# A decode kernel's layer crossing: half of a further V chunk kept on chip for each batch row, a key ring of 24 KB in place of 32 KB, and other places for the loads around it

## The chip, the cores and the metric

The kernel runs on one core of a Trainium2 chip. The metric is the device time of one execution in microseconds, the median of several runs of the same program. All data is float32.

## The reference

Two layers. Each adds to `x` (2 batch rows of one token, 512 channels) an attention over a cache, and then a small mixing MLP:

```python
x = x + _A_ref(_layernorm(x), A_k_cache, A_v_cache, A_wq, A_wo)
x = x + _B_ref(_layernorm(x), B_w1, B_b1, B_w2, B_b2)
# and both lines once more, on the same caches and weights
def _A_ref(x, k_cache, v_cache, wq, wo):      # Hq 32, Hkv 8, Sk 32768, Dh 128
    q = heads of (x @ wq);  k, v = each cached head for 4 query heads
    p = softmax(q k^T * Dh ** -0.5)
    return (p v) @ wo
def _B_ref(x, w1, b1, w2, b2):                # one token, F = 1792
    return w2 * gelu(w1 * layernorm(x) + b1) + b2
```

A cached head of one batch row is 32768 x 128 floats, 16.8 MB, in K and again in V. There are 16 such pairs. The second layer reads the same caches with other queries, and its queries need the whole result of the first layer for that batch row. So nearly everything is read from memory twice.

## The kernel before, in words

**Units and chunks.** A unit is one (layer, batch row, KV head); there are 32. Its K and its V are each eight chunks of 2 MB (16 KB in each of the 128 partitions), and a chunk is eight quads (256 KB, 2 KB per partition). For each K chunk TensorE makes scores (`scores`, L483), eight matmuls; after the last chunk the row maximum is taken (L498, L506, L508, L512), ScalarE makes the exponentials (L523, L540), and TensorE multiplies them with V (`acc`, L640), again eight matmuls for a chunk. TensorE takes each float32 matmul in two passes, so the trace shows 16 matmul records for a chunk where the program's list has eight instructions.

**Memory.** One tile `mem` holds everything that is streamed: cells of 16 KB per partition, numbered from 0, one chunk to a cell. Cells 9 to 12 are shared with the projection weights; behind cell 12 lie five further quads (`REST`, "cell 13"). Every cache load is one DMA that `load` (L191) puts on the single queue of SyncE (SP), in a fixed order written by the kernel's own planner. A load waits on SP for the last reader of the cell that it overwrites, and all later loads stand behind it.

**Units around the crossing.** Head 7 is the keeper. The order of the units there is, as (layer, batch row, head):

- unit 13 = `N1`: (0, 0, 7), the last of layer 0 for row 0
- unit 14 = `N1 + 1`: (0, 1, 5)
- unit 15 = `N1 + 2`: (1, 0, 7)
- unit 16 = `N2`: (0, 1, 7), the last of layer 0 for row 1
- unit 17 = `N2 + 1`: (1, 0, 5)
- unit 18 = `N3`: (1, 1, 7); unit 19: (1, 1, 5)

After unit 13 layer 0 is complete for row 0. While K of unit 14 streams, the mixer of row 0 is computed, chiefly on DVE and ACT (14 gelu tiles, `hidden_sum`), with a few products on TensorE (`mix_2` L755, `mix_3` L919, `to_columns` L366), and then the queries of unit 15 (`q_products`, L397, one product for each quarter of the channels). This is the first crossing. The second is the same for row 1, under K of unit 17. During a crossing the stream brings K alone.

**What stays on chip.** K chunks 0 to 2 of the keeper stay in cells 0 to 2 from layer 0 to layer 1. Of its V, `KEPT` names the places: chunks 1, 2, 3 in cells 8 to 10, chunks 5, 6, 7 in cells 3 to 5, and five quads of chunk 4 in cell 13 (three more of its quads go through PSUM). Chunk 0 is read again in layer 1. Both rows use the same places, one after the other.

**The ring.** With so much held, K of units 14 and 17 has two cells, 6 and 7. It is loaded in half chunks (four quads, 1 MB) into four slots of half a cell: 32 KB per partition in all. A load waits until TensorE has read the half chunk four before it. TensorE keeps this order, half chunk by half chunk, and between them come the mixer's products, the query products and idle products (`idle_products`, L799): matmuls of the identity, in sets of three, whose result nobody reads. V of the two units goes the same way for its first two chunks.

**Places.** Outside of the ring, `spread`, `buffer` and `half` choose a free cell for a load: the one that gives it the most time between its last reader and its own issue. `FOLLOWS` and `BETWEEN` are keys that place V chunks among the K chunks of the next unit in the load order.

## Time and profile before

| | |
|---|---|
| median of 3 runs | 2501.42 us (2501.13 to 2503.52) |
| the profiled execution | 2503.54 us, its span 2501.7 us |
| read from memory | 1061.19 MB, 424 GB/s over the span |
| busy share of the span | PE 57%, PE weight loads 16%, DVE 10%, ACT 7% |
| first crossing (K of unit 14) | about 1130 to 1190 us of the span |
| second crossing (K of unit 17) | about 1310 to 1370 us |

The page cuts the span into 40 slices of 62.5 us and gives for each the busy share of the 16 DMA engines and what they moved; the windows do the same for chosen stretches. In the timeline a row is a run of like instructions on one engine: its start, its length, the line, and in brackets the idle time ahead of it with what ended it.

### The profile page before, as it was taken

Reading aid. Unit: us, or ns where it says so; the run is one execution under the profiler, and the core shown is the slowest. Engines: PE = TensorE matmul, PEld = TensorE weight load, DVE = VectorE, ACT = ScalarE, POOL = GpSimd, SP = SyncE. Lnnn points to the kernel's source line nnn. Section 1 sums busy time; section 2 is a strip of 40 time slices with the busy share of each in tenths; the row PEclk is TensorE's granted clock in tenths of the full one; section 3 lists DMA queues with packets and bytes.
Section 4 is the critical chain, followed back from the end, with each engine's and each line's share of the span. In section 5 each row is a group of like instructions: output and inputs, shape, how many; then the busy total and the mean of one; then the engine's idle time right before and its main releaser. Section 6 shows DMA issues by size and latency. Waiting matters only on the chain.

```text
span 2501.7 us, 20938 instructions
## 1 busy us (share of the span) xinstructions
PE 1425.7 (57%) x9478; PEld 393.0 (16%) x9478; DVE 256.5 (10%) x659; ACT 185.5 (7%) x544; POOL 4.9 (0%) x17
## 2 busy tenths in 40 slices
PE   4544645546545545658578675455555565456546
PEld 1111111111111111113123111111111111111112
DVE  1000000000000000003123110000000000010002
ACT  0000000000000000002012000000000000012002
POOL 0000000000000000000000000000000000000000
PEclk8777677776777777879889888777777777777778
DMA  9999999999999999989999999999999999999996
GB/s 420 435 433 428 437 434 433 431 433 431 434 434 428 434 435 432 424 348 418 427 423 415 424 429 432 432 433 433 434 430 431 435 431 432 432 434 434 427 434 283
DMA packets 30882, 1062.54 MB, mean 425 GB/s; under 512 B 3781, under 2 KB 3785, under 8 KB 4426
## 3 DMA queue, kind: packets, MB, share of 16 engines
q1 hardware_dynamic: 30504, 1061.17, 98.7%
q8 instruction: 74, 1.21, 0.2%
q14 instruction: 14, 0.11, 0.0%
q10 hardware_dynamic: 290, 0.04, 0.0%
HBM read 1061.19 MB, written 0.00 MB: 424 GB/s over the span
## 4 chain that ended last, share of the span: by engine, by line
DMA 72%; PE 26%; issue 0%; another core or an unknown queue 0%; DVE 0%; ACT 0%; SPq 0%; ACTq 0%
DMA mem<-in_v_dram 60%; PE acc L640 19%; DMA mem<-in_kt_dram 11%; PE scores L483 3%; DMA mem<-in_wqo_dram 2%; PE kept L164 1%; PE kept L397 1%; PE small L799 1%; PE small L512 0%; PE small L671 0%; PE bcast L397 0%; PE kept L298 0%; SPq L191 0%; PE small L506 0%
## 5 line engine op out<-in xcount | busy, mean ns | idle before, releaser
L483 PE MATMUL scores<-mem,small_sb 128*32 128x512 f32 x4096 | 618.5, 725 | 549.1 <-DMA mem<-in_kt_dram 549.1
L640 PE MATMUL acc<-mem,S 128*16 128x512 f32 x4088 | 617.3, 736 | 469.5 <-DMA mem<-in_v_dram 465.9
L483 PEld LDWEIGHTS scores<-mem,small_sb 128*32 128x32 f32 x4096 | 147.3, 127 | 922.5 <-issue 838.4
L523 ACT ACTIVATE S<-S,small_sb 128x128 f32<-128x128 f32 x232 | 119.3, 518 | 1967.5 <-DVE small_sb L514 1378.6
L640 PEld LDWEIGHTS acc<-mem,S 128*16 128x16 f32 x4088 | 131.2, 109 | 829.2 <-issue 693.3
L498 DVE TENSOR_REDUCE small_sb<-scores 128x1 f32<-128x512 f32 x64 | 44.2, 691 | 755.0 <-PE scores L483 755.0
L518 DVE STREAM_TRANSPOSE S<-scores 128x512 f32<-128x512 f32 x64 | 45.5, 710 | 144.2 <-PE acc L640 140.0
L397 PE MATMUL kept<-mem,small_sb 128*2 128x512 f32 x96 | 52.8, 671 | 4.3 <-DMA mem<-in_wqo_dram 2.6
L298 PE MATMUL kept<-mem,small_sb 128*1 128x512 f32 (+1 forms) x236 | 43.1, 612 | 2.7 <-ACT mem L894 2.4
L523 ACT ACTIVATION_READ_ACCUMULATOR S<-S,small_sb 128x1 f32 x232 | 43.3, 187 | 0.0
L508 DVE TENSOR_REDUCE small_sb<-small 1x4 f32<-1x128 f32 x32 | 8.9, 279 | 282.1 <-PE small L506 282.1
L673 DVE RECIPROCAL small_sb<-small 128x4 f32<-128x4 f32 x32 | 5.9, 185 | 301.0 <-PE small L671 301.0
L682 DVE TENSOR_TENSOR small_sb<-small,small_sb 128x4 f32<-128x4 f32 x31 | 5.1, 164 | 293.9 <-PE small L680 293.9
L610 DVE SCALAR_TENSOR_TENSOR S<-acc,small_sb,S 128x128 f32<-128x128 f32 x93 | 32.6, 351 | 3.3
L894 ACT ACTIVATE S<-bcast,small_sb 128x512 f32<-128x512 f32 x28 | 21.6, 778 | 86.4 <-DVE small_sb L763 84.3
L799 PE MATMUL small<-small_sb 128*128 128x128 f32 x160 | 25.1, 297 | 1.0 <-DVE small_sb L371 1.0
L608 DVE TENSOR_SCALAR S<-acc,small_sb 128x128 f32<-128x128 f32 x31 | 10.8, 350 | 143.1 <-PE acc L640 143.1
L164 PE MATMUL kept<-mem,small_sb 48*2 48x512 f32 x32 | 25.3, 934 | 0.0
L423 PE MATMUL small<-small_sb,mem 2*128 2x2 f32 x112 | 14.7, 249 | 17.9 <-DVE mem L419 17.9
L799 PEld LDWEIGHTS small<-small_sb 128*128 128x128 f32 x160 | 21.0, 199 | 16.6 <-issue 15.4
L397 PE MATMUL bcast<-mem,small_sb 128*1 128x512 f32 (+1 forms) x40 | 20.3, 633 | 0.0
L680 PEld LDWEIGHTS small<-small_sb,S 128*128 128x128 f32 x62 | 12.5, 252 | 47.3 <-issue 39.7
(154 smaller groups left out, 348.0 us busy)
## 6 DMA issues: line engine op xcount, KB each, us to landing
mem<-in_kt_dram SPq DMA_DIRECT2D x12, 4096.0 KB
mem<-in_v_dram SPq DMA_DIRECT2D x23, 2048.0 KB
mem<-in_v_dram SPq DMA_DIRECT2D x9, 4096.0 KB
mem<-in_kt_dram SPq DMA_DIRECT2D x32, 1024.0 KB
mem<-in_kt_dram SPq DMA_DIRECT2D x12, 2048.0 KB
mem<-in_wqo_dram SPq DMA_DIRECT2D x4, 3840.0 KB
mem<-in_wqo_dram SPq DMA_DIRECT2D x3, 4096.0 KB
mem<-in_kt_dram SPq DMA_DIRECT2D x2, 6144.0 KB
```

What stands on the lines that cost most here:

```text
L164: nc.tensor.matmul(q_ps[n][:B, :], low[:, j * B : (j + 1) * B], lowered[h][:, j * D : (j + 1) * D], start=(j == 0), stop=False,)
L298: nc.tensor.matmul((rows if to is None else to)[32 * g : 32 * g + b + 1, :], weights if b else weights[:, 1:], row, start=to is not None, ...
L397: nc.tensor.matmul(q_ps[n][:m, :], xnT[:, d, b : b + m], wq_at(h, d), start=(d == 0 and h not in lowered), stop=(d == last),)
L423: nc.tensor.matmul(pt[:, r * m : (r + 1) * m], q_row[n][:m, r * DH : (r + 1) * DH], ident[:m, :m], start=True, stop=True,)
L483: nc.tensor.matmul(sc_ps[n, half][32 * g : 32 * g + 32, :], q, kc[k * NG + g], start=(i == 0 and k == 0), stop=(i == PACK - 1 and k == SUB ...
L498: nc.vector.tensor_reduce(mx[n][:, half : half + 1], sc_ps[n, half], axis=AX.X, op=ALU.max)
L518: nc.vector.transpose(S[half], sc_ps[n, half])
L523: nc.scalar.activation(s[:, :, h], s[:, :, h], AF.Exp, bias=neg[n][:, h : h + 1], scale=SCALE, accum_out=lsum[n][:, half, h : h + 1],)
L610: nc.vector.scalar_tensor_tensor(t, acc[:, k * DH : (k + 1) * DH], mask[:, k : k + 1], t, op0=ALU.mult, op1=ALU.add)
L640: nc.tensor.matmul(acc[32 * g : 32 * g + R * QT, :], S[half][:, col : col + R * QT], vc[q], start=(c == v_from[n] and q < NG), stop=(c == ...
L799: nc.tensor.matmul(p[:, :P], ident, ident, start=True, stop=True)
L894: nc.scalar.activation(hid[key, f], px[key], AF.Gelu_apprx_tanh, bias=shift[key][:, f : f + 1], scale=slope[key][:, f : f + 1],)
```

## The change

- `KEPT` becomes `KEPT_V`, one table for each row. Both get an entry for chunk 0: four of its eight quads stay in the upper half of cell 7. For row 0 the chunks 1 to 3 now stay in cells 3 to 5 and the chunks 5 to 7 in cells 8 to 10; row 1 has them as before.
- The ring for K of units 14 and 17 (`ring_quads`, a new function) is four slots of three quads (768 KB each), from cell 6 to the middle of cell 7: 24 KB per partition. A K group of 32 quads is loaded as ten pieces of three and one of two. Eleven quads of V go through it too; the other five of V chunk 1 go to cell 0.
- `PLACE_K` and a longer `PLACE_V` fix the cells of loads in units 13 to 20, which were chosen by the rules. K of units 16 and 19 is loaded one chunk at a time at its start (before: three chunks in one, or two).
- `FOLLOWS` and `BETWEEN` move some V chunks in the load order.
- The four query products of the next unit stand 1, 2, 1 behind three half chunks (before: 2, 2 behind two), and the copy of the query row comes half a chunk later. Of the eight sets of idle products in each crossing the three earliest stay.

SP's loads at the first crossing. Rows are groups of like DMAs; 128x2048 is four quads, 128x1536 three, 128x4096 a whole chunk. Before:

```order
L191 DMA mem<-in_v_dram 128x8192
L191 DMA mem<-in_v_dram 128x4096
L191 DMA mem<-in_v_dram 128x12288
L191 DMA mem<-in_v_dram 128x2560
L191 DMA mem<-in_v_dram 128x1536
L191 DMA mem<-in_v_dram 128x4096 x3
L191 DMA mem<-in_kt_dram 128x2048 x16
L191 DMA mem<-in_v_dram 128x2048 x4
L191 DMA mem<-in_v_dram 128x4096 x3
```

Now:

```order
L196 DMA mem<-in_v_dram 128x8192
L196 DMA mem<-in_v_dram 128x2048 x2
L196 DMA mem<-in_v_dram 128x12288
L196 DMA mem<-in_v_dram 128x2560
L196 DMA mem<-in_v_dram 128x1536
L196 DMA mem<-in_v_dram 128x4096 x3
L196 DMA mem<-in_kt_dram 128x1536 x10
L196 DMA mem<-in_kt_dram 128x1024
...
L196 DMA mem<-in_v_dram 128x1536 x3
L196 DMA mem<-in_v_dram 128x1024
L196 DMA mem<-in_v_dram 128x2560
L196 DMA mem<-in_v_dram 128x4096 x3
```

V chunk 0 of unit 13 comes in two halves, one of which stays; the 16 half chunks of K have become two times eleven pieces (the second eleven are like the first), and V of unit 14 follows in four pieces and a rest.

PE in the first crossing, from `mix_2` to the end of K. Rows are groups of matmuls; `scores` x4 is half a chunk. Before:

```order
L755 MATMUL bcast<-S_91,small_sb 128x512
L483 MATMUL scores<-mem,small_sb 32x512 x12
L799 MATMUL small<-small_sb 128x128 x3
L483 MATMUL scores<-mem,small_sb 32x512 x4
L799 MATMUL small<-small_sb 128x128 x3
...
L919 MATMUL bcast<-S_91,small_sb 128x512
L799 MATMUL small<-small_sb 128x128 x3
L483 MATMUL scores<-mem,small_sb 32x512 x4
L366 MATMUL small<-small_sb,S_91 128x1 x4
L799 MATMUL small<-small_sb 128x128 x3
L483 MATMUL scores<-mem,small_sb 32x512 x4
L397 MATMUL bcast<-mem,small_sb 1x512 x2
L799 MATMUL small<-small_sb 128x128 x3
L483 MATMUL scores<-mem,small_sb 32x512 x4
L397 MATMUL bcast<-mem,small_sb 1x512 x2
L799 MATMUL small<-small_sb 128x128 x3
```

Now:

```order
L797 MATMUL bcast<-S_91,small_sb 128x512
L518 MATMUL scores<-mem,small_sb 32x512 x16
L841 MATMUL small<-small_sb 128x128 x3
...
L961 MATMUL bcast<-S_91,small_sb 128x512
L518 MATMUL scores<-mem,small_sb 32x512 x4
L398 MATMUL small<-small_sb,S_91 128x1 x4
L518 MATMUL scores<-mem,small_sb 32x512 x4
L429 MATMUL bcast<-mem,small_sb 1x512
L518 MATMUL scores<-mem,small_sb 32x512 x4
L429 MATMUL bcast<-mem,small_sb 1x512 x2
L518 MATMUL scores<-mem,small_sb 32x512 x4
L429 MATMUL bcast<-mem,small_sb 1x512
```

The first four half chunks after `mix_2` stand bare (before: three), then three half chunks have a set of idle products behind them (one of them is shown), and behind `mix_3` there are none.

SP behind the last V load of unit 14 (the first row), between the crossings. Before:

```order
L191 DMA mem<-in_v_dram 128x4096
L191 DMA mem<-in_kt_dram 128x4096 x2
L191 DMA mem<-in_kt_dram 128x12288
L191 DMA mem<-in_v_dram 128x4096
L191 DMA mem<-in_kt_dram 128x4096
L191 DMA mem<-in_kt_dram 128x8192 x2
```

Now:

```order
L196 DMA mem<-in_v_dram 128x4096
L196 DMA mem<-in_kt_dram 128x4096 x5
L196 DMA mem<-in_v_dram 128x2048
L196 DMA mem<-in_kt_dram 128x4096
L196 DMA mem<-in_kt_dram 128x8192 x2
```

The first two of the K loads are the last of unit 15; then K chunks 0 to 2 of unit 16, in one before and now in three; then V chunk 0 of unit 15, now half of it; then K chunk 3 of unit 16. That last load goes to cell 10 by `PLACE_K`; before, the rule gave it cell 7, and the next load (chunks 4 and 5) cells 3 and 4.

The diff, cut to what the text speaks of:

```diff
-KEPT = {1: (8, 8), 2: (8, 9), 3: (8, 10), 4: (5, 13), 5: (8, 3), 6: (8, 4), 7: (8, 5)}
+KEPT_V = (
+    {0: (4, 7.5), 1: (8, 3), 2: (8, 4), 3: (8, 5), 4: (5, 13), 5: (8, 8), 6: (8, 9), 7: (8, 10)},
+    {0: (4, 7.5), 1: (8, 8), 2: (8, 9), 3: (8, 10), 4: (5, 13), 5: (8, 3), 6: (8, 4), 7: (8, 5)},
+)
-PLACE_V = {(1, 7): 1}
+PLACE_K = {(0, 6): 5, (2, 3): 0, (2, 4): 2, (2, 5): 0, (2, 6): 2, (2, 7): 6, (3, 3): 10, (3, 4): 3, (3, 6): 5, ...}
+PLACE_V = {(1, 2): 1, (1, 3): 2, (1, 4): 6, (1, 5): 1, (1, 6): 6, (1, 7): 1, (2, 0): 7, (2, 4): 8, ...}
-FOLLOWS = {2: (2.2, -0.9, -0.8, -0.7, 3.5, -0.6, -0.5, -0.4), 5: (3.05, 0.1, 0.2, 0.3, 5.1, 3.1, 3.2, 3.3)}
+FOLLOWS = {2: (2.2, -0.9, -0.8, -0.7, 3.5, -0.6, -0.5, -0.4), 5: (3.05, -0.9, -0.8, -0.7, 5.1, 3.1, 3.2, 3.3)}
-BETWEEN = (1.1, 1.2, 1.3, 2.1, 2.2, 3.1, 4.1, 5.1)
+BETWEEN = (2.1, 2.2, 2.3, 2.4, 2.5, 3.1, 4.1, 5.1)
+RING0, RING_SLOTS, RING_QUADS, RING_V = 6, 4, 3, 11
...
+    def ring_quads(n, is_v, c, count=JT // QT):
+        layer, b, h = unit_of(n)
+        c0, size = next(g for g in GROUPS if g[0] <= c < sum(g))
+        own = ring.setdefault((n, is_v, c0), [])
+        end = min(size * (JT // QT), RING_V if is_v else NCH * JT)
+        w = QT * P
+        a = piece(v if is_v else kt, b * HKV + h, c0, size)
+        while len(own) < (c - c0) * (JT // QT) + count:
+            f, slot = len(own), turns[0] % RING_SLOTS
+            turns[0] += 1
+            m = min(RING_QUADS, end - f)
+            k = RING0 * (JT // QT) + slot * RING_QUADS
+            t = mem[:, k * w : (k + m) * w]
+            load(t, a[:, f * w : (f + m) * w])
+            until = (v_done if is_v else k_done)[n, c0 + (f + m - 1) // (JT // QT)]
+            for j in range(k // NG, -(-(k + m) // NG)):
+                busy[j] = max(busy[j], until)
+            own += quads(t)
+        return own[(c - c0) * (JT // QT) :][:count]
...
+        elif n in (N1 + 1, N2 + 1):
+            k_at[n, c] = ring_quads(n, False, c)
+            return
         elif limit == RING:
-            bufs = spread(m, until, n in (N1 + 1, N2 + 1) and m == 1)
+            bufs = spread(m, until, False, PLACE_K.get((n - N1, c)))
...
-            loads = ((0, 3), (3, 1), (4, 2), (6, 2)) if n in (N1, N2) else ((0, 2), (2, 2), (4, 2), (6, 2))
+            loads = ((0, 3), (3, 1), (4, 2), (6, 2)) if n == N1 else ((0, 2), (2, 2), (4, 2), (6, 2))
+            if n in (N2, N3 + 1):
+                loads = (*((c, 1) for c in range(NG)), (4, 2), (6, 2))
...
-                q2 = mixed[layer - 1, b] + 0.5
-                q3 = q2 + 1
+                q2 = mixed[layer - 1, b] + 1
+                q3 = q2 + 0.5
...
-            for k in range(2, 2 * (NCH - 3)):
-                at(kend - 0.5 * k - 0.5, idle_products, KEEP_UP, rank=3)
+            for k in range(7, 2 * (NCH - 3)):
+                at(kend - 0.5 * k, idle_products, KEEP_UP, rank=3)
...
-            at(q, q_products, n + 1, 0, 1)
-            at(q + 0.5, q_products, n + 1, 2, 3)
+            at(q, q_products, n + 1, 0)
+            at(q + 0.5, q_products, n + 1, 1, 2)
+            at(q + 1, q_products, n + 1, 3)
```

More of the change, by code (lines that the diff above doesn't have):

```diff
@@ L192, in load, with buffer @@
         loaded[0] += t.shape[-1] / CK
[L194 to L196 removed]
+    def buffer(m, limit, until, place=None):
+        ks = range(0, limit - m + 1, m) if place is None else [place]
+        k = min(ks, key=lambda k: (-room(k, m, until), idle(k, m)))
         assert idle(k, m) <= now[0]
@@ L199, in buffer, with half @@
         return cells(k, m)
-    def half(until):
-        k = min((k / 2 for k in range(2 * WCELL0)), key=lambda k: (-fit(k, 0.5, until), idle(k, 0.5)))
+    def half(until, place=None):
+        ks = [k / 2 for k in range(2 * WCELL0)] if place is None else [place]
+        k = min(ks, key=lambda k: (-fit(k, 0.5, until), idle(k, 0.5)))
         assert fit(k, 0.5, until) >= 1
@@ L225, in spread @@
         k = min(ks, key=lambda k: (-fit(k, m, until), idle(k, m)))
-        if fit(k, m, until) >= 2 and not parted:
+        if (place is not None or fit(k, m, until) >= 2) and not parted:
+            assert idle(k, m) <= now[0] and fit(k, m, until) >= 1, (now, k, m, until, fit(k, m, until), lead(k, m), idle(k, m))
             hold(k, m, until)
@@ L576, in load_v @@
                 return
-            bufs = [half(until)[:, : CK - f]]
+            bufs = [half(until, PLACE_V.get((n - N1, c)) if layer else None)[:, : CK - f]]
+        elif n in (N1 + 1, N2 + 1) and c * (JT // QT) < RING_V:
+            at = ring_quads(n, True, c, min(JT // QT, RING_V - c * (JT // QT)))
+            f = len(at) * w
+            bufs = [cells(0)[:, : CK - f]] if f < CK else []
+            if bufs:
+                assert idle(0) <= now[0]
+                hold(0, 1, until)
         elif limit == RING:
```

24 lines of the change are left out of this document (13 added, 11 removed).

## The prediction

> **What bounds the kernel now.** I read the page first: the slices, the queues, the chain.
>
> ```profile
> DMA  9999999999999999989999999999999999999996
> GB/s 420 435 433 428 437 434 433 431 433 431 434 434 428 434 435 432 424 348 418 427 423 415 424 429 432 432 433 433 434 430 431 435 431 432 432 434 434 427 434 283
> q1 hardware_dynamic: 30504, 1061.17, 98.7%
> DMA 72%; PE 26%; issue 0%; another core or an unknown queue 0%; DVE 0%; ACT 0%; SPq 0%; ACTq 0%
> ```
>
> One queue is busy for 98.7% of the span and carries nearly all the bytes. The end is therefore set by two things: how many bytes there are at which rate, and the moments at which the queue has nothing to do. The moments lie in slices 18 to 23, around the two crossings; the rest runs at 430 or more. TensorE counts only where it lets a load go late. So I looked at windows there, the first row being the undisturbed stream:
>
> ```profile
> 500.00:950.00 450.00, 239.53 (x1562) 62.71 (x1554) 31.86 (x91) 23.66 (x88) 0.00 (x0) 0.75 1.00 433
> 1100.00:1120.00 20.00, 8.58 (x51) 2.45 (x51) 2.04 (x6) 3.62 (x10) 0.00 (x0) 0.74 0.50 216
> 1130.00:1165.00 35.00, 26.25 (x170) 9.75 (x170) 11.13 (x22) 8.25 (x11) 0.54 (x1) 0.85 1.00 420
> 1320.00:1355.00 35.00, 26.32 (x184) 9.76 (x177) 14.46 (x27) 10.01 (x13) 0.54 (x1) 0.90 1.01 419
> 1180.00:1200.00 20.00, 14.75 (x117) 4.96 (x120) 7.31 (x15) 1.38 (x3) 0.00 (x0) 0.90 1.00 389
> 1360.00:1380.00 20.00, 19.50 (x142) 7.49 (x142) 7.01 (x17) 1.39 (x3) 0.54 (x1) 1.00 1.00 394
> 1565.00:1570.00 5.00, 1.21 (x16) 0.23 (x12) 0.85 (x2) 0.00 (x0) 0.00 (x0) 0.81 0.95 380
> 1555.00:1565.00 10.00, 5.70 (x36) 1.23 (x32) 0.00 (x0) 0.00 (x0) 0.00 (x0) 0.66 1.02 437
> ```
>
> The last column is GB/s, the one ahead of it the DMA share. Large loads go at 433; the ring's half chunks at 420 with the engines full, so that rate belongs to the piece. The queue stands still for 10 us before 1120 (share 0.50 of 20 us). Behind the rings it loses 20 x (420 - 389) / 420 = 1.5 us and 20 x (420 - 394) / 420 = 1.2 us, and at 1565 5 x (437 - 380) / 437 = 0.65 us.
>
> **Bytes.** Half of V chunk 0 stays on chip for both rows.
>
> ```profile
> mem<-in_v_dram SPq DMA_DIRECT2D x23, 2048.0 KB
> mem<-in_kt_dram SPq DMA_DIRECT2D x32, 1024.0 KB
> ```
>
> A chunk of 2048 KB is 2.097 MB, 4.84 us at 433. Two halves fewer are 2.097 MB: **-4.84 us**. Against it, pieces get smaller. The two V chunks that now come in halves pay the step from 433 to 420: 4.2 MB, 0.3 us. For pieces of 768 KB no window stands alone. From 2 MB to 1 MB a piece cost 3%; if the same step came again at 768 KB it would be 13 GB/s on 2 x 16.8 MB, 2.5 us; nothing if the rate depends on the row of a partition only below that size. A quarter less is nearer to no step: I take 0.2 us. Bytes together: **-4.3 us** (-4.8 to -2.0).
>
> In a sentence that the sum can do without: the Trainium skill, DMA: Bandwidth & Descriptors, gives a load 2.0 us and its bytes at 436 GB/s, with the advice to make loads of 1 MiB at least; were that paid in a row, a K unit of the ring would go from 16 x 4.4 = 70 us to some 82. Here 1 MB pieces flow at 420, 2.5 us each, so the fixed part lies under the transfers queued ahead, as long as there are such.
>
> **The hole before 1120.**
>
> ```profile
> 1108.00:1110.00 2.00, 0.00 (x0) 0.00 (x0) 0.00 (x0) 0.00 (x0) 0.00 (x0) 0.50 0.74 319
> 1110.00:1112.00 2.00, 0.00 (x0) 0.00 (x0) 0.00 (x0) 0.00 (x0) 0.00 (x0) 0.50 0.06 25
> 1112.50 3.62 PE L640 MATMUL acc<-mem,S 128*16 128x512 f32 x16 [9.90 <-DMA mem<-in_v_dram]
> 1118.58 1.05 PE L701 MATMUL small<-small_sb,mem 128*128 128x2 f32 x8 [0.82 <-DVE mem L712]
> 1119.70 2.34 SPq L191 DMA_DIRECT2D mem<-in_v_dram  x5
> 1119.70:1121.20 1.50, 1.24 (x10) 0.54 (x14) 0.40 (x3) 0.00 (x0) 0.00 (x0) 0.93 0.45 96
> 1121.20:1121.70 0.50, 0.50 (x8) 0.19 (x4) 0.00 (x0) 0.00 (x0) 0.00 (x0) 0.50 0.65 205
> ```
>
> The load into cell 13 waits until `fold_rows` (L701) has read that cell. In the new order the same load stands at the same place behind the same products: **0**. The rows also give the price of a restart: after the issue at 1119.70 the stream misses (433 - 96) / 433 x 1.5 + (433 - 205) / 433 x 0.5 = 1.4 us.
>
> **The ring.** A load waits for the piece four before it. Four slots of 1 MB are 4 x 2.5 = 10 us of transfer; with 0.75 MB they are 7.5 us, and behind the piece in use only three are on the way: 5.6 us in place of 7.5. TensorE's lag is what uses this up:
>
> ```profile
> 1174.04 1.07 PE L483 MATMUL scores<-mem,small_sb 128*32 128x512 f32 x8
> 1174.92 1.88 PE L397 MATMUL bcast<-mem,small_sb 128*1 128x512 f32 x4
> 1176.73 0.94 PE L799 MATMUL small<-small_sb 128*128 128x128 f32 x6
> 1177.60 1.07 PE L483 MATMUL scores<-mem,small_sb 128*32 128x512 f32 x8
> 1178.48 1.88 PE L397 MATMUL bcast<-mem,small_sb 128*1 128x512 f32 x4
> 1180.29 0.94 PE L799 MATMUL small<-small_sb 128*128 128x128 f32 x6
> 1181.15 1.92 PE L483 MATMUL scores<-mem,small_sb 128*32 128x512 f32 x16
> ```
>
> From 1174.04 to 1181.15 two half chunks take 3.56 us each, while one arrives every 2.5: a lag of 2.1 us from this alone, and the stall of 1.2 to 1.5 follows. Now the queries stand 1, 2, 1 without idle products: 2.0, 2.9 and 2.0 us by the same rows, so they add 0.4 us of lag. The cover is 1.9 us thinner, the lag about 1.7 us smaller; the stall stays near 1. A half chunk also straddles two pieces, which frees the first earlier. I take **-0.5 us per crossing, -1.0** (from -2.7, both gone, to +2, where the thinner cover is short at every piece until the DMA engines stand in line).
>
> **A gain behind the second crossing.** The load that comes late at 1565 had one load of 4096 KB (9.7 us) queued between its reader's data and itself; in the new places there are two (19.4 us): **-0.65**.
>
> **A new wait.** K chunk 3 of unit 16 now goes to cell 10, where V chunk 7 of row 0 stays. Its last reader is unit 15's V, the last of six resident chunks:
>
> ```profile
> 1249.09 1.92 PE L483 MATMUL scores<-mem,small_sb 128*32 128x512 f32 x16 [1.14 <-DMA mem<-in_kt_dram]
> 1252.02 0.38 PE L506 MATMUL small<-small_sb 128*1 128x128 f32 x2 [1.00 <-DVE small_sb L504]
> 1257.21 3.63 PE L640 MATMUL acc<-mem,S 128*16 128x512 f32 x32
> 1263.59 3.63 PE L640 MATMUL acc<-mem,S 128*16 128x512 f32 x32
> 1265.56 0.33 SPq L191 DMA_DIRECT2D mem<-in_kt_dram  x1
> ```
>
> At 1249.09 the last K chunk of unit 15 has landed. The maximum, the exponentials and six chunks follow, and the sixth ends at 1263.59 + 3.63 = 1267.2: 18.1 us later. Before, K chunks 4 and 5 waited for the fifth (issue at 1265.56, 16.5 us later), with 24.2 us queued ahead: three K chunks, V chunk 0 and K chunk 3, five of 4.84. Now the waiting load is K chunk 3 itself, and ahead of it are three K chunks and half of V chunk 0: 3.5 x 4.84 = 16.9 us. So the queue is dry at 16.9, the issue comes at 18.1, and with 1.4 us of restart the loss is 2.6 us. The queue's engines do not run dry together (the share was 0.74 in the two microseconds from 1108, 0.06 in the next two), which adds up to 2. I take **+3.5** (0, if fewer products come before the reader than I count, to 4.6). Behind the load stand K 4 to 7 of unit 16 and the ring; TensorE has the three chunks to work on and loses nothing more. The same products at the low clock,
>
> ```profile
> 1444.50 3.64 PE L640 MATMUL acc<-mem,S 128*16 128x512 f32 x16
> 1449.32 3.63 PE L640 MATMUL acc<-mem,S 128*16 128x512 f32 x32
> ```
>
> take up to 3.64 for a chunk, not 1.8 (the first row, between the second crossing and unit 18's V): with two chunks of them the wait is 3.6 longer, +7.1. The other loads that were given places have two chunks or more queued between the data of their reader and themselves, 9.7 us, most three; a reader takes 1.8 to 3.64, twice that with another's products ahead: **0**, and their single K loads for unit 16 and 19 cost at most the step already counted.
>
> **The sum.** -4.3 - 1.0 - 0.65 + 3.5 = -2.5 us. The profiled execution took 2503.54 us with a span of 2501.7, so it becomes 2499.2 and 2501.0; it lies 2.1 us over the median of the runs, so the forecast for the median is 2501.42 - 2.5 = **2498.9 us**. What a measurement can tell from no change is about 0.2%, 5 us: 2496.4 to 2506.4 is no change.
>
> **Rivals.**
>
> A. *The wait at cell 10 is hidden, or smaller.* Then -4.3 - 1.0 - 0.65 = -6.0, 2495.4; with the ring's stalls gone as well -7.7, 2493.7. For it: the margin missed is only 1.2 us ahead of the restart. Against it: 18.1 us is read from rows of the same products at the high clock, and 16.9 us from the order of the loads. Chance 0.25.
>
> B. *The clock falls under K of the crossings* (the slower side). The rows show it in the second one:
>
> ```profile
> 1344.39 1.07 PE L483 MATMUL scores<-mem,small_sb 128*32 128x512 f32 x8 [1.42 <-DMA mem<-in_kt_dram]
> 1346.88 1.94 PE L483 MATMUL scores<-mem,small_sb 128*32 128x512 f32 x8 [1.42 <-DMA mem<-in_kt_dram]
> 1348.74 1.65 PE L799 MATMUL small<-small_sb 128*128 128x128 f32 x6
> 1353.47 1.07 PE L483 MATMUL scores<-mem,small_sb 128*32 128x512 f32 x8
> ```
>
> Two gaps of 1.42 us, and the matmuls take 1.94 in place of 1.07 for 6.6 us. Now one more half chunk stands bare there, and five sets of idle products are gone. At the low clock a half chunk with idle products takes 3.6, with two query products 1.94 + 3.4 (1.88 scaled by 1.94 / 1.07) = 5.3, with one 3.6, against 2.5 of arrival. One such stretch over the three sets costs 3 x 1.1 = 3.3 us; staying low through the queries adds 1.1 + 2.8 + 1.1 = 5.0. The 24 KB ring has no cover for either. At both crossings 3.3 to 8.3 us, without the ring's gain: -4.3 - 0.65 + 3.5 + 2 x (3.3 to 8.3) = +5.2 to +15.2: 2506.6 to 2516.6, the middle 2511.6. It decides from 3.3 us per crossing on. Against it: behind `mix_3` nearly every half chunk has a product of its own behind it, and a bare one at the low clock (1.94) still fits 2.5. Chance 0.13. The Trainium skill, TensorE: Matmul & The Clock Gate, on HAM oscillation, asks for a gap of over some 3.4 us before the clock falls; by that the bare halves would be safe and B would have no ground, but the row at 1346.88 shows the low clock after gaps of 1.42.
>
> C. *The low clock meets the new wait*, at +7.1 in place of 3.5: +1.1, 2502.6, or with stalls at every piece of the ring (+2 for -1) +4.1, 2505.5. For it: the second crossing's V shows such chunks; against it: the first one's does not. Chance 0.14.
>
> D. *Each further piece pays a fixed part*, at most the restart of 1.4 us: six pieces more of K in each crossing are 8.4 us, both 16.8, 2515.7. Against it: 420 GB/s at 1 MB with a full queue. Chance 0.03. (This is the way of the rule from DMA: Bandwidth & Descriptors in the Trainium skill, told above.)
>
> The forecast has the other 0.45; its own range is 2496 to 2502. That the half chunk isn't spared is excluded by the order of the loads, which has 128x2048 where 128x4096 stood.
>
> **How the numbers follow.** Faster: nearly all of A and 0.03 of the forecast's low end, 0.27. Slower: B and D, 0.15, and 0.02 of C, 0.17. No change 0.56. The range goes from A's middle down to its end, 2493.5, and up past C to the near end of B, 2507.5; outside are some 0.05 below and 0.14 above.
>
> **What would show it.** Bytes: 1059.1 MB read. New wait: a gap in the DMA share of some 3 us about 17 us behind unit 15's last K, its load released by `acc`. Ring: windows behind it at 395 or more. 1565: no dip. The hole of 10 us unchanged. B: `scores` of 1.94 over long stretches of K in the crossings. I am wrong if there is no gap at unit 16's K chunk 3, or if the ring loses more than 3 us.

## The result, and the profile after

The changed kernel takes 2519.24 us (median of 6 runs, 2517.08 to 2520.89), the kernel before 2502.61 (6 runs): a ratio of 1.0066, 95% interval 1.0056 to 1.0076. It is 0.66% slower. 2498.9 was forecast, no change the likeliest, and 2507.5 was the upper end of the range.

The page of the changed kernel, its GB/s in 40 slices and its bytes:

```profile
GB/s 419 434 436 428 436 432 434 435 428 436 431 431 431 431 433 433 428 349 360 428 377 387 402 430 433 435 434 433 430 432 426 433 431 432 433 434 430 432 436 285
HBM read 1059.10 MB, written 0.00 MB: 420 GB/s over the span
```

The 2.09 MB are saved. Four slices that stood at 418, 423, 415 and 424 stand at 360, 377, 387 and 402. Windows around the first crossing, the stretch between the crossings and the second crossing (the last column is GB/s, the one ahead of it the DMA share), of the kernel before:

```profile
1130.00:1225.00 95.00, 69.88 (x460) 23.38 (x464) 25.06 (x49) 14.25 (x20) 1.08 (x2) 0.87 1.00 416
1225.00:1320.00 95.00, 70.29 (x488) 19.17 (x484) 15.18 (x40) 8.51 (x28) 0.00 (x0) 0.84 1.00 429
1320.00:1425.00 105.00, 81.78 (x536) 26.92 (x528) 27.48 (x54) 14.26 (x20) 1.08 (x2) 0.89 1.01 416
```

and of the changed kernel, with two short windows in the filled part of its rings:

```profile
1130.00:1225.00 95.00, 70.17 (x410) 20.05 (x410) 25.14 (x49) 14.24 (x20) 1.09 (x2) 0.87 0.97 383
1225.00:1320.00 95.00, 67.97 (x446) 17.52 (x446) 14.80 (x38) 8.52 (x28) 0.00 (x0) 0.83 0.92 388
1320.00:1425.00 105.00, 78.69 (x472) 22.14 (x476) 25.79 (x51) 14.25 (x20) 1.08 (x2) 0.84 0.99 392
1143.00:1150.00 7.00, 6.14 (x41) 1.76 (x44) 1.57 (x5) 0.00 (x0) 0.00 (x0) 1.00 1.01 415
1346.00:1353.00 7.00, 6.20 (x43) 1.66 (x42) 1.57 (x5) 0.00 (x0) 0.00 (x0) 1.00 1.01 413
```

In time at the stream's 433 GB/s: 95 x (416 - 383) / 433 = 7.2 us in the first crossing, 95 x (429 - 388) / 433 = 9.0 between, 105 x (416 - 392) / 433 = 5.8 in the second. Together 22.0; less 4.84 for the bytes, 17.2. The spans differ by 2519.0 - 2501.7 = 17.3. So, by this sum, everything lies in these three stretches.

**Between the crossings** it is the load at cell 10. Rows of the changed kernel's timeline, TensorE's and SP's, and after them three windows:

```profile
1257.20 3.52 PE L518 MATMUL scores<-mem,small_sb 128*32 128x512 f32 x16 [2.71 <-DMA mem<-in_kt_dram]
1264.10 3.47 PE L682 MATMUL acc<-mem,S 128*16 128x512 f32 x16 [0.27 <-ACT S L575]
1274.90 3.63 PE L682 MATMUL acc<-mem,S 128*16 128x512 f32 x32
1278.59 0.80 SPq L196 DMA_DIRECT2D mem<-in_kt_dram  x2
```

```profile
1257.20:1279.00 21.80, 19.51 (x142) 5.26 (x146) 4.98 (x13) 2.90 (x10) 0.00 (x0) 0.85 0.64 271
1270.00:1282.00 12.00, 11.37 (x106) 3.15 (x102) 0.83 (x4) 2.17 (x8) 0.00 (x0) 1.00 0.30 104
1274.00:1281.00 7.00, 7.00 (x70) 2.12 (x66) 0.18 (x1) 0.00 (x0) 0.00 (x0) 1.00 0.22 56
```

The last K chunk of unit 15 has landed at 1257.2, V chunk 7 is read until 1278.5, and the load goes out at 1278.59, 21.4 us later, not 18.1: the K chunk and the first V chunk take 3.52 and 3.47 us, where the kernel before took 1.92 and 1.91. By the 16.9 us of transfers counted behind the K chunk, the queue would have gone dry 4.5 us earlier. The windows show it dry sooner. From 1257.2 to 1279 it moved 271 GB/s, which is 5.9 MB or 13.6 us of the stream; the count was 3.5 chunks, 7.3 MB. So 1.4 MB of these loads had been moved before TensorE began the K chunk, and the queue was short from about 1270. From there to 1282 it lost 12 x (433 - 104) / 433 = 9.1 us, which is all of the loss of this stretch.

**In the crossings** the pieces flow at 415 and 413 while the queue is full, but it doesn't stay full. Pieces of three quads straddle the half chunks of four: every second one holds quads of two half chunks. One place in the first crossing where such a piece is held, by the timeline, and a window behind it:

```profile
1163.09 1.92 PE L518 MATMUL scores<-mem,small_sb 128*32 128x512 f32 x2 [0.19 <-DMA mem<-in_kt_dram]
1164.94 0.94 PE L841 MATMUL small<-small_sb 128*128 128x128 f32 x6
1165.80 1.07 PE L518 MATMUL scores<-mem,small_sb 128*32 128x512 f32 x8
1166.90 0.33 SPq L196 DMA_DIRECT2D mem<-in_kt_dram  x1
```

```profile
1168.00:1170.00 2.00, 2.00 (x16) 0.96 (x12) 0.46 (x1) 0.47 (x2) 0.00 (x0) 1.00 0.82 292
```

The row of two at 1163.09 is one quad, the last of a half chunk; it had waited for its data until then. The other two quads of its piece belong to the next half chunk, behind idle products. The slot comes free 3.8 us after the data came, and the stream has a hole (292 GB/s). Some 0.9 us of the 3.8 are the low clock, which fell here for a moment: from 1161 to 1165 the granted clock was 0.57. The same in the second crossing, at the high clock:

```profile
1363.62 1.06 PE L518 MATMUL scores<-mem,small_sb 128*32 128x512 f32 x6 [0.29 <-DMA mem<-in_kt_dram]
1365.51 1.05 PE L518 MATMUL scores<-mem,small_sb 128*32 128x512 f32 x2 [0.83 <-DMA mem<-in_kt_dram]
1366.48 0.94 PE L841 MATMUL small<-small_sb 128*128 128x128 f32 x6
1367.35 1.07 PE L518 MATMUL scores<-mem,small_sb 128*32 128x512 f32 x8
```

Here the slot is free 2.9 us after the data. The rows also show that a half chunk that comes in two parts is taken in two goes, each as long as a whole one: 1.06 us for three quads, 1.05 for the fourth, 1.07 for all four together. With a piece that is a half chunk, the slot is free some 1.1 us after the data.

### The profile page after: what moved, and what is told of

It is laid out like the page before. It is cut to its first block, busy times and chain, and to the rows that moved or that the text cites. A ratio compares the mean times of both kernels' runs of the same rounds, so it can differ in the third digit from the quotient of the medians.

```text
span 2519.0 us, 20852 instructions
## 1 busy us (share of the span) xinstructions
PE 1422.7 (56%) x9418; PEld 387.1 (15%) x9418; DVE 256.6 (10%) x659; ACT 185.5 (7%) x544; POOL 4.9 (0%) x17
## 3 DMA queue, kind: packets, MB, share of 16 engines
HBM read 1059.10 MB, written 0.00 MB: 420 GB/s over the span
## 4 chain that ended last, share of the span: by engine, by line
DMA 72%; PE 26%; DVE 0%; issue 0%; ACT 0%; another core or an unknown queue 0%; SPq 0%; ACTq 0%
DMA mem<-in_v_dram 60%; PE acc L682 19%; DMA mem<-in_kt_dram 11%; PE scores L518 4%; DMA mem<-in_wqo_dram 2%; PE kept L169 1%; PE kept L429 0%; PE small L547 0%; PE small L713 0%; PE bcast L429 0%; PE small L541 0%; ACT mem L915 0%; ACT S L558 0%; PE small L743 0%
## 5 line engine op out<-in xcount | busy, mean ns | idle before, releaser
L518 PE MATMUL scores<-mem,small_sb 128*32 128x512 f32 x4096 | 642.2, 729 | 570.1 <-DMA mem<-in_kt_dram 569.9
L682 PE MATMUL acc<-mem,S 128*16 128x512 f32 x4088 | 624.5, 739 | 470.6 <-DMA mem<-in_v_dram 466.7
L455 PE MATMUL small<-small_sb,mem 2*128 2x2 f32 x112 | 15.2, 253 | 17.9 <-DVE mem L451 17.9
L541 PE MATMUL small<-small_sb 128*1 128x128 f32 x64 | 16.9, 358 | 4.0 <-DVE small_sb L539 4.0
L455 PEld LDWEIGHTS small<-small_sb,mem 2*128 2x128 f32 x112 | 14.0, 192 | 30.6 <-DVE mem L451 27.3
L953 DVE SCALAR_TENSOR_TENSOR acc<-S,small_sb,acc 128x512 f32<-128x512 f32 x24 | 18.1, 755 | 2.5
```

The source lines that it names most:

```text
L455: nc.tensor.matmul(pt[:, r * m : (r + 1) * m], q_row[n][:m, r * DH : (r + 1) * DH], ident[:m, :m], start=True, stop=True,)
L518: nc.tensor.matmul(sc_ps[n, half][32 * g : 32 * g + 32, :], q, kc[k * NG + g], start=(i == 0 and k == 0), stop=(i == PACK - 1 and k == SUB ...
L682: nc.tensor.matmul(acc[32 * g : 32 * g + R * QT, :], S[half][:, col : col + R * QT], vc[q], start=(c == v_from[n] and q < NG), stop=(c == ...
L953: nc.vector.scalar_tensor_tensor(h if f == FT - 1 else acc, h, w, acc, op0=ALU.mult, op1=ALU.add)
```

## The experiments

All runs have the kernel before beside them; its median there was 2502.0 to 2502.3 us. For each run the GB/s of the same three windows follow, and in brackets the time that these mean against 433 (window x (433 - GB/s) / 433). The quoted spans are those of one profiled execution, so the windows tell where, the medians how much.

| run | median us | ratio, 95% | first crossing | between | second crossing |
|---|---|---|---|---|---|
| before | 2502.61 | | 416 (3.7) | 429 (0.9) | 416 (4.1) |
| changed | 2519.24 | 1.0066 (1.0056 to 1.0076) | 383 (11.0) | 388 (9.9) | 392 (9.9) |
| unswap | 2512.39 | 1.0037 (1.0022 to 1.0052) | 391 (9.2) | 421 (2.6) | 386 (11.4) |
| ring4x4 | 2502.15 | 1.0000 (0.9990 to 1.0009) | 421 (2.6) | 406 (5.9) | 424 (2.2) |
| ring4x4old | 2504.96 | 1.0012 (1.0003 to 1.0021) | 418 (3.3) | 403 (6.6) | 419 (3.4) |
| ring5x3n | 2508.44 | 1.0021 (1.0011 to 1.0031) | 412 (4.6) | 411 (4.8) | 413 (4.8) |
| ring6x2 | 2504.85 | 1.0008 (0.9999 to 1.0018) | 412 (4.6) | 391 (9.2) | 417 (3.9) |
| ring3x4 | 2512.47 | 1.0040 (1.0026 to 1.0053) | 406 (5.9) | 401 (7.0) | 397 (8.7) |
| ring4a | 2512.07 | 1.0040 (1.0024 to 1.0055) | 397 (7.9) | 392 (9.0) | 410 (5.6) |
| ring5x2 | 2518.38 | 1.0065 (1.0051 to 1.0079) | 385 (10.5) | 408 (5.5) | 390 (10.4) |
| idle8 | 2517.67 | 1.0061 (1.0046 to 1.0076) | 387 (10.1) | 390 (9.4) | 389 (10.7) |
| idle0 | 2515.94 | 1.0054 (1.0040 to 1.0067) | 385 (10.5) | 392 (9.0) | 388 (10.9) |
| both6x2 | 2498.71 | 0.9988 (0.9979 to 0.9997) | 415 (3.9) | 416 (3.7) | 418 (3.6) |
| both4a | 2505.62 | 1.0016 (1.0007 to 1.0024) | 388 (9.9) | 427 (1.3) | 408 (6.1) |
| best2 | 2500.47 | 0.9993 (0.9985 to 1.0002) | 413 (4.4) | 421 (2.6) | 416 (4.1) |
| six | 2502.13 | 1.0000 (0.9991 to 1.0009) | 401 (7.0) | 428 (1.1) | 408 (6.1) |

### The wait at cell 10: unswap

Row 0's kept chunks go back to the cells of before; cell 10 then holds chunk 3, which is read three chunks sooner.

```diff
-    {0: (4, 7.5), 1: (8, 3), 2: (8, 4), 3: (8, 5), 4: (5, 13), 5: (8, 8), 6: (8, 9), 7: (8, 10)},
+    {0: (4, 7.5), 1: (8, 8), 2: (8, 9), 3: (8, 10), 4: (5, 13), 5: (8, 3), 6: (8, 4), 7: (8, 5)},
```

> The changed kernel, with row 0's kept V chunks back in the cells of before (1 to 3 in cells 8 to 10, 5 to 7 in cells 3 to 5), so that the load that waits at cell 10 waits for V chunk 3 of unit 15 and not for chunk 7: three chunks of products earlier, some 6 us. Theory W (the wait at cell 10 is a loss of its own, about 9 us of empty queue in the changed kernel's trace): the gap near 1280 us goes, the time falls by 7 to 9 us to 2510 to 2512. Rival M (the wait only moves, to the loads of K chunks 4 to 7, which now wait for V chunks 5 to 7): a gap of 3 us or more opens at those loads, and the time falls by less than 5 us. Rival R (all of the loss comes from the rings, and the gap is refilled later): the same time within 2 us.

2512.39 us, 6.9 less than the changed kernel. Its window between the crossings, and the issue of the load:

```profile
1225.00:1320.00 95.00, 70.52 (x474) 18.80 (x478) 14.79 (x38) 8.51 (x28) 0.00 (x0) 0.82 1.00 421
```

```profile
1268.77 0.33 SPq L196 DMA_DIRECT2D mem<-in_kt_dram  x1
```

421 for 388, 7.2 us by the windows: W holds in the main, the wait is a loss of its own. A rest of 1.7 us against before is left; the first V chunk of unit 15 still ran at the low clock there, 3.54 us. The rings stay as late as they were (391 and 386).

### Idle products: idle8 and idle0

```diff
-            for k in range(7, 2 * (NCH - 3)):                      # changed kernel: 3 sets
-                at(kend - 0.5 * k, idle_products, KEEP_UP, rank=3)
+            for k in range(2, 2 * (NCH - 3)):                      # idle8: 8 sets
+                at(kend - 0.5 * k - 0.5, idle_products, KEEP_UP, rank=3)
+            for k in range(10, 2 * (NCH - 3)):                     # idle0: none
```

> The changed kernel with the eight sets of idle products of before put back in each crossing, behind the same half chunks as before. Theory C (each 0.94 us of products between two half chunks delays the next load by as much, and there is no cover for it): the rings lose 1 to 3 us more each, the time rises by 2 to 6 us, 2521 to 2525. Rival I (the clock falls without them): scores of 1.94 us for half a chunk go from the rings, which lose 3 us less each or better, and the time falls by 6 us or more, to 2513.

> The changed kernel without the three sets of idle products that were left in each crossing. Theory S says that a straddling piece waits for whatever stands between two half chunks, so without the sets the three halves there free their pieces 0.9 us earlier: the rings lose 1 to 2 us less each, 2515 to 2517, if the clock stays up. If the clock falls there (half chunks of 1.9 us in place of 1.07), the rings lose as much or more: 2519 to 2525. With eight sets it was 2517.7.

2517.67 with eight sets, 2519.24 with three, 2515.94 with none: the intervals overlap, and in each of the three the crossings stand at 383 to 392. Rival I falls: the idle products that were taken away did not make the rings late. Theory C's 2 to 6 us for the return of the eight sets are not there either. The median of idle0 lies where S put it, but its windows show no gain in the crossings. The clock falls for a few microseconds with any number of sets, where the half chunks stand bare: granted 0.57 from 1161 to 1165 with three, 0.59 from 1156.9 to 1161 with eight, 0.57 from 1358 to 1362 with none. Without any set it also falls later; idle0, at the end of K in the first crossing:

```profile
1184.31 1.92 PE L518 MATMUL scores<-mem,small_sb 128*32 128x512 f32 x2 [1.85 <-DMA mem<-in_kt_dram]
1186.16 1.86 PE L455 MATMUL small<-small_sb,S 1*128 1x1 f32 x8
```

One quad takes 1.92 us here, 1.05 at the high clock, and L455 takes 1.86 us, 1.05 in the changed kernel. What the sets cost in one place they may give back in another; that isn't shown.

### A ring of 32 KB: ring4x4 and ring4x4old

```diff
-    {0: (4, 7.5), 1: (8, 3), ...
+    {1: (8, 3), ...                                    # both rows: chunk 0 is read again
-RING0, RING_SLOTS, RING_QUADS, RING_V = 6, 4, 3, 11
+RING0, RING_SLOTS, RING_QUADS, RING_V = 6, 4, 4, 11
```

`ring4x4old` has in addition eight sets of idle products, two pairs of query products and the copy half a chunk earlier, as before.

> The changed kernel without the kept half of V chunk 0 (it is read again), and with that room given to the ring: four slots of four quads, 32 KB. Places, query products and idle products as in the changed kernel. Theory C (the thinner cover of 24 KB makes the rings late: 7 us in the first, 6 us in the second beyond what was lost before): the rings lose 1 to 3 us each again; bytes cost 4.3 us more, and the load at cell 10 has 2.4 us more ahead of it: 2519 - 13 + 4.3 - 2.4 = about 2508 us. Rival I (the rings are late because idle products were taken away and the clock falls, whatever the slots hold): the rings lose 6 us or more each as in the changed kernel, and the time is 2519 + 4.3 - 2.4 = about 2521 us.

> The changed kernel without the kept half, with a ring of four slots of four quads (as in the run of that kind before), and also with the eight sets of idle products and the two pairs of query products of before. What differs from the kernel before is then the places, V behind the ring and the order of a few V loads. If the new order of the query products and the missing idle products are what keeps the 32 KB ring in time (it lost some 1 us in a crossing, against 2 before), the rings lose 2 us each again and the time is 2504 to 2505; if the places did it, it stays at 2502.

```profile
1130.00:1225.00 95.00, 67.65 (x438) 20.13 (x442) 25.07 (x49) 14.26 (x20) 1.08 (x2) 0.87 1.01 421
1320.00:1425.00 105.00, 78.28 (x520) 22.86 (x512) 27.96 (x55) 14.26 (x20) 1.08 (x2) 0.90 1.01 424
1250.00:1290.00 40.00, 35.34 (x256) 10.16 (x248) 9.51 (x23) 2.89 (x10) 0.00 (x0) 0.88 0.90 381
```

With the 32 KB ring the crossings are at 421 and 424, better than before (416 both), although the wait at cell 10 is still there (381 around it): 2502.15, level with before and 17.1 us under the changed kernel. The expectation of 2508 was too high, since the rings lose less than they did before. So the ring is the larger cause. ring4x4old is 2.8 us slower, with 418 and 419: the new order of the query products, the later copy and the fewer idle products together look like a small gain with a ring that has the room, though the two intervals overlap a little.

### The cut or the size: ring6x2, ring3x4, ring5x3n, ring5x2, ring4a

`ring4x4` differs from the changed kernel in two ways: more room, and pieces that are half chunks. These runs part them. A step of TensorE's order is a half chunk, four quads; pieces of two or four quads never reach from one half chunk into the next, pieces of three do (the straddle).

```diff
-RING0, RING_SLOTS, RING_QUADS, RING_V = 6, 4, 3, 11
+RING0, RING_SLOTS, RING_QUADS, RING_V = 6, 6, 2, 11     # ring6x2,  24 KB
+RING0, RING_SLOTS, RING_QUADS, RING_V = 6, 3, 4, 11     # ring3x4,  24 KB
+RING0, RING_SLOTS, RING_QUADS, RING_V = 6, 5, 3, 11     # ring5x3n, 30 KB, chunk 0 is read again
+RING0, RING_SLOTS, RING_QUADS, RING_V = 6, 5, 2, 11     # ring5x2,  20 KB
+RING0, RING_SIZES, RING_V = 6, (4, 2, 2, 4), 11         # ring4a,   24 KB, slots of these quads
```

> The changed kernel with the same 24 KB cut into six slots of two quads (512 KB loads). Behind the piece in use five are on the way: 6.3 us of transfers in place of 5.6, and no half chunk of TensorE's order straddles two pieces with a quad left over. Theory C (cover decides): the rings lose 3 to 5 us each in place of 9.1 and 8.0, the time falls by 6 to 10 us, 2509 to 2513. Rival P (smaller pieces pay a fixed part each, or 4 KB rows go slower): the stream in the filled part of the ring falls under 410 GB/s and the time is the same or up to 6 us longer.

> The changed kernel with the same 24 KB as three slots of four quads: 1 MB loads that are the half chunks of TensorE's order, but only two of them behind the piece in use, 5.0 us of transfers (5.6 with four slots of three quads, 6.3 with six of two). Theory C (the transfers queued behind the piece in use decide): the rings lose more than the 9 and 8 us of the changed kernel, 2522 us or more. Rival S (the straddle decides: pieces of three quads end in the middle of half chunks, so that a piece waits for the products that stand behind a half chunk): the rings lose 2 to 5 us each, 2508 to 2513.

> The changed kernel without the kept half, with a ring of five slots of three quads, 30 KB. Behind the piece in use four are on the way, 7.5 us, the same as with four slots of four quads, which took 2502.15 us and lost 0.9 and 0.3 us in the rings; only the cut differs: pieces of three quads end inside half chunks. Theory C (the transfers on the way decide): 2501 to 2504, the rings lose 1 us each. Rival S (the straddle decides): the rings lose 3 us or more each, 2507 or more.

> The changed kernel with a ring of only 20 KB, five slots of two quads: 5.1 us of transfers behind the piece in use, less than the changed kernel's 5.6, but no straddle. Theory C: the rings lose more than the changed kernel's 9 and 8 us, 2520 or more. Rival S: the rings lose 2 to 4 us each, a little more than with six slots (2504.85), 2506 to 2510. With both at work: in between.

> The changed kernel with the same 24 KB ring, still four slots, but of 4, 2, 2 and 4 quads: 21 loads for a unit's K in place of 22, on average 5.6 us of transfers behind the piece in use (5.0 behind one of four quads, 6.3 behind one of two), as with four slots of three; no piece ends inside a half chunk. Theory S (the straddle is the larger part of the 9.1 and 7.8 us that the rings lose): the rings lose 2 to 4 us each, the time is 2506 to 2510. Theory C (the few transfers on the way): 7 us or more each, 2516 or more.

ring6x2, at 2504.85, came out better than either of its theories allowed. Its stream is under 410 GB/s, as P said, but it isn't slower for that. ring3x4 lies at S's 2508 to 2513 and far from C's 2522, though its rings lose 5.9 and 8.7 us, more than S allowed. ring5x3n is where S put it.

Two pairs with equal transfers on the way tell the straddle. The first is ring5x3n against ring4x4 (its crossings stand above). Behind the piece in use are four pieces of three quads in ring5x3n and three of four in ring4x4, 7.5 us each. The windows of ring5x3n:

```profile
1130.00:1225.00 95.00, 68.81 (x430) 19.77 (x434) 25.16 (x49) 14.26 (x20) 1.09 (x2) 0.91 1.00 412
1320.00:1425.00 105.00, 80.33 (x520) 23.64 (x516) 28.03 (x55) 14.25 (x20) 1.08 (x2) 0.96 1.00 413
```

It loses 9.4 us in the crossings where ring4x4 loses 4.8, and its median is 6.3 us higher. Some 1.2 us of either difference is the lower rate of pieces of 768 KB (415 and 413 against 420 on two K units). The second, ring4a against the changed kernel (four slots and 5.6 us on the way in both):

```profile
1130.00:1225.00 95.00, 66.55 (x418) 20.04 (x422) 25.11 (x49) 14.24 (x20) 1.08 (x2) 0.88 1.00 397
1320.00:1425.00 105.00, 78.65 (x500) 22.12 (x500) 26.41 (x52) 14.24 (x20) 1.08 (x2) 0.91 1.01 410
```

13.5 us where the changed kernel loses 20.9, and 7.2 us less in the median. So the straddle costs some 3 to 7 us over both crossings, in rings of either size. The number of loads isn't the cause: ring6x2 has more of them and is faster. Note that ring4a's pieces of two quads do end inside a half chunk, other than its expectation says; what they don't do is reach into the next one. How the straddle costs its time is read from the held pieces above, and the runs bear it out in part only: idle0 took the idle products from between the half chunks, and its crossings didn't gain.

The room tells as well: without straddle, ring4x4 (7.5 us on the way) loses 4.8 us, ring4a (5.6) 13.5 and ring3x4 (5.0) 14.6. ring6x2 has six slots of the same 24 KB, 6.3 us on the way, and loses 8.5, part of which is not lateness: its pieces of 512 KB go at 397 and 401 with the engines full (404 and 407 in both6x2, which has the same ring),

```profile
1150.00:1175.00 25.00, 22.88 (x108) 6.63 (x108) 14.45 (x27) 12.86 (x17) 1.08 (x2) 1.00 1.02 397
1350.00:1375.00 25.00, 23.50 (x116) 6.62 (x112) 12.82 (x22) 12.85 (x17) 0.54 (x1) 1.00 1.02 401
```

which is 2 us on a K unit of 16.8 MB against 420. Neither theory stands alone: S asked for 2 to 4 us in a crossing of ring4a, and there are 7.9 and 5.6; C asked for 2516 or more of ring4a, and for the time of ring4x4 from ring5x3n. Both act.

ring5x2 came out at 2518.38, but it doesn't test what it was made for. It has a wait of its own: its last V piece, one quad, goes to a slot that V holds, and V is multiplied only after the exponentials. Its timeline, and then SP's waits from 1185 to 1200 (us in total, times, longest):

```profile
1193.67 1.90 PE L682 MATMUL acc<-mem,S 128*16 128x512 f32 x16
1194.72 1.28 SPq L196 DMA_DIRECT2D mem<-in_v_dram  x3
```

```profile
SPq L196 <- PE acc L682: 7.6, 2, 6.5
```

SP stood 6.5 us for `acc` there. `six` below has the same ring with ten quads of V, without that piece.

### Both repairs, and what they allow: both6x2, both4a, best2, six

`both6x2` is ring6x2 with unswap's table, `both4a` ring4a with it. `best2` is both6x2 with K chunk 3 of unit 16 moved on to cell 9; `six` is best2 with a ring of 20 KB and six quads kept:

```diff
-PLACE_K = {..., (3, 3): 10, ...}
+PLACE_K = {..., (3, 3): 9, ...}                          # best2, six
+RING0, RING_SLOTS, RING_QUADS, RING_V = 6, 5, 2, 10      # six
-    {0: (4, 7.5), 1: (8, 8), ...                         # both rows
+    {0: (6, 7.25), 1: (8, 8), ...                        # six
```

> Both repairs together: row 0's kept V chunks in the cells of before, and the 24 KB ring as six slots of two quads. If the wait at cell 10 and the rings are separate losses, they add up: 2504.85 (six slots) less 6.8 (what the cells gave, 2519.2 - 2512.4) = 2498.0 us, 2496 to 2500, which is faster than the kernel before by 2 to 6 us. If the one shift only moves the other's wait, the sum falls short: 2501 or more.

> The slots of 4, 2, 2 and 4 quads together with the cells of before for row 0's kept V chunks. If S holds, 2519.2 less 10 to 13 (rings) less 6.8 (the wait at cell 10) = 2499 to 2502; larger pieces than in the six slots of two (2498.7) go at a higher rate, but with fewer transfers on the way. If C holds, 2509 or more.

> Six slots of two quads, row 0's kept V chunks in the cells of before, and K chunk 3 of unit 16 in cell 9 instead of cell 10, where V chunk 2 of row 0 stays, so that its load waits for the second resident chunk and not the third, 1.8 to 3.6 us earlier. The 2.2 us that the run without this last step still lost there go: 2498.7 - 2 = 2496.5 us, 2495 to 2498.5. If that residue had another cause, 2498.7 as before.

> As the run with cell 9, but the ring is 20 KB, five slots of two quads, ten quads of V go through it, and the room gained keeps six quads of V chunk 0 on chip for each row in place of four: 1.05 MB less to read, 2.4 us. If five slots of two quads keep time nearly as six do, 2494 to 2496.5; if the ring's cover of 5.1 us is too thin, the rings lose 3 us more each and it is 2499 or more.

both6x2, at the same 1059.10 MB as the changed kernel:

```profile
1130.00:1225.00 95.00, 73.50 (x430) 20.67 (x434) 25.06 (x49) 14.25 (x20) 1.09 (x2) 0.91 1.01 415
1225.00:1320.00 95.00, 69.73 (x473) 17.98 (x471) 14.76 (x38) 8.50 (x28) 0.00 (x0) 0.80 0.98 416
1320.00:1425.00 105.00, 84.81 (x520) 24.16 (x512) 27.97 (x55) 14.25 (x20) 1.08 (x2) 0.95 1.02 418
```

2498.71, 20.5 us under the changed kernel and faster than the kernel before, if by little: 0.9988 (0.9979 to 0.9997). The two losses add up: 2504.85 - 6.85 = 2498.0. both4a adds up too: 2512.07 - 6.85 = 2505.2 against 2505.62, which is neither S's 2499 to 2502 nor C's 2509. Of the saved bytes both6x2 keeps most: the crossings cost what they cost before, and the stretch between them 2.8 us more.

That rest is the wait at cell 10 once more, since the queue again runs dry sooner than 16.9 us after the last K chunk of unit 15 has landed. In both6x2:

```profile
1250.20 3.64 PE L518 MATMUL scores<-mem,small_sb 128*32 128x512 f32 x16 [1.69 <-DMA mem<-in_kt_dram]
1265.36 0.33 SPq L196 DMA_DIRECT2D mem<-in_kt_dram  x1
1264.00:1266.00 2.00, 1.42 (x18) 0.24 (x12) 0.14 (x1) 1.83 (x8) 0.00 (x0) 1.00 0.28 115
```

The load goes out 15.2 us after the landing, and by the count it would have had 1.7 to spare; but from 1264, 13.8 after the landing, the queue moves 115 GB/s.

best2 was meant to take that rest away. The stretch between goes from 3.7 to 2.6 us of loss, but the median is 2500.47, within the range of both6x2's runs and above their median: no gain can be told. six reads 1058.05 MB, and its ring of 20 KB gives back all of that: 401 and 408 in the crossings, 2502.13.

## Why the prediction was wrong

**What bounds the kernel** was read rightly: bytes, their rate, and the moments when the queue is dry. The 17.3 us are such moments, but for some 1.2 us of lower rate.

**Bytes.** -4.84 is right. The step for pieces of 768 KB was set at 0.2 us; 415 and 413 in place of 420 make it 16.8 MB x (1/415 - 1/420) and x (1/413 - 1/420), 0.5 and 0.7 us, 1.2 together, inside its bounds.

**The hole before 1120** stayed as it was: from 1060 to 1130 both kernels read at 360 GB/s. **The load at 1565** comes in time: at the same place, 17 us later, the window 1582 to 1587 of the changed kernel has no dip.

```profile
1582.00:1587.00 5.00, 1.28 (x12) 0.12 (x4) 0.85 (x2) 0.00 (x0) 0.00 (x0) 1.00 1.15 498
```

**The new wait** was found at its place, with its load, its reader and its sign, but the term of +3.5 was mis-sized: 9.0 by the windows, 6.9 by the run that takes it away. Two things were wrong in it, 3.3 us each. The products before the reader were priced at the high clock. Rival C had the low clock, at 3.6 us, and the rows show 3.2 (3.52 and 3.47 for 1.92 and 1.91); the issue came 21.4 us after the landing in place of 18.1. And the queue lasted 13.6 us from the landing, not 16.9: the prediction counted every load behind the K chunk as still to come, but 1.4 MB of them had been moved by then (13.8 us in both6x2). 21.4 - 13.6 is 7.8, and with the 1.4 for the restart 9.2. The up to 2 us that the prediction allowed for engines running dry one by one would be a part of the second 3.3. Why later loads are so far on at a landing isn't shown.

**The ring** is the step that failed, and in its sign: -0.5 us per crossing was forecast, +7.2 and +5.8 came (with 0.5 and 0.7 for the lower rate of the pieces in them). Two sentences carried it. "A half chunk also straddles two pieces, which frees the first earlier" is the wrong way round. The straddling piece keeps its slot until TensorE has taken the next half chunk, past whatever stands between: 2.9 and 3.8 us after its data in the rows above, where a half chunk of its own takes 1.1. The pairs ring5x3n/ring4x4 and ring4a/changed put 3 to 7 us on the straddle. And "the cover is 1.9 us thinner, the lag about 1.7 us smaller" set the lag of one moment, the query products, against a cover that is needed at every piece. The trace of before shows a ring that is on time nearly everywhere and late once; from that I took the margin at the late moment, but not how small it was elsewhere. Its upper bound, +2, rested on the thought that the engines of the queue fall into line once and the loss ends; in the changed kernel it does not end: from 1150 to 1195 no stretch of 5 us reaches 400 GB/s, where the kernel before stands at 418 to 421 up to 1180.

**Rival B** had the side right and the cause wrong. The loss in the crossings, 7.2 and 5.8 us, lies inside its 3.3 to 8.3, by luck: idle8 and idle0 show that the sets don't matter, half chunks in the crossing stand mostly at 1.07, and the short low stretch is there with any number of sets. The time itself, 2519.24, is above even B's upper end of 2516.6. For the rule of the Trainium skill that was set against it (TensorE: Matmul & The Clock Gate, HAM oscillation: over some 3.4 us of gap before the clock falls), the row of idle0 at 1184.31 again shows slow matmuls behind a gap of 1.85: from 1184 to 1190 the granted clock was 0.50. **Rival D**, 1.4 us for each further load, is refuted by ring6x2: pieces half as large as the 1 MB pieces and twice as many, and 14.4 us faster than the changed kernel. (The fit of the Trainium skill that the prediction set beside D, in DMA: Bandwidth & Descriptors, Anatomy of one DMA, was measured on loads that GpSimd issues. Here SyncE issues them, and behind each other in a full queue pieces of 512 KB went at 397 to 407 GB/s.) **Rival A** didn't come: the wait at cell 10 was larger than forecast, not smaller.

What is still open: how much of the remaining loss of ring4a (13.5 us in its crossings, 7.8 in before) is the room alone and how much the order of the products in it; no run held one and varied the other at 24 KB. That idle products are without effect is shown only in the straddling ring.

## What to carry to other kernels

Cut the loads of a ring so that none reaches from one step of the consumer into the next: such a load holds its slot through everything that the consumer does between the two steps, and the ring of this kernel lost more in its crossings, 13 us, than the bytes saved, 4.8; some 3 to 7 of the 13 go with the cut, the rest with the smaller room and the lower rate of its pieces. Price a ring by its worst release at every slot, landing to free, against the transfers behind it, and count a thinner cover as lost time until the trace shows slack everywhere; smaller pieces buy cover back at a lower rate. Where a load is moved to a buffer with a later reader, price the reader's chain at the low clock too, and take the time at which the queue runs dry from the bytes that it moves, not from the landing of the load ahead: here 1.4 MB of the later loads had been moved by then.

## What the runs showed of the hardware

The rate of a full queue falls with the size of its loads, and with it of a partition's row (no run parts the two): 433 GB/s in the long loads, 420 for loads of 1 MB (rows of 8 KB), 415 and 413 for 768 KB (6 KB), 397 to 407 for 512 KB (4 KB). That the step from 1 MB to 768 KB is small and the next one larger was not expected; even so the finer ring was the better one.

When TensorE could start on a chunk, up to 1.4 MB of the loads queued behind it had already been moved (at 1257.2 in the changed kernel; the queue then lasted 13.6 us where the bytes counted are 16.9, and 13.8 at the same place in both6x2). At that place a wait that by count left the queue dry for 4.5 us cost 9.1.

Score products for one quad took as long as those for four: 1.05 us for 2 records, 1.07 for 8. So a half chunk that is taken in two goes keeps TensorE twice as long.
